# One more chunk of a sum kernel without transposes on TensorE, and two transform visits moved forward

## The chip, the cores and the metric

One core of a Trainium2 chip. The metric is the device time of one execution in microseconds; lower is better. TensorE is written PE (its weight loads PEld), VectorE DVE, ScalarE ACT, GpSimd POOL. SP only issues DMA transfers.

## The reference

Everything is float32, S = 2048 rows, D = 448 columns, F = 1792. Cut to what is computed:

```python
xn = layernorm(A_q)
# branch A: a state space layer
k_shift = sum_t k_pad[:, t:t+S] * shift_k[:, 3-t]      # 4 taps along the rows
kv = k_shift * v
y = irfft(rfft(kv, 2S) * rfft(ssm_k, 2S))[:S] + kv * ssm_D   # long convolution
a = xn * y
# branch B: an MLP
b = mish(xn @ w1 + b1) @ w2
out = A_q + a + b
```

## The kernel before

**The MLP.** The rows are cut into 8 chunks of 256, the 1792 features into 7 pairs of 128. One step of the MLP is a chunk and a pair: the first product g1_mm (22 matmuls, line 545) gives h transposed in PSUM, ACT makes Mish of it (L553), ACT and DVE split it into a rounded part and a residue (`ach`, L90; `acl`, L91), and two steps later the second product g2_mm (12 matmuls, L577 to L579) adds it to the chunk's two sums in PSUM. Each float32 product is made of three products of rounded parts, hence the many "hi" and "lo" tiles: `w1h`, `w1l`, `w2h`, `w2l`, `XH`, `XL`. When a chunk is done, DVE takes its sums out of PSUM (L584); the pool of these sums has two buffers, so the next chunk's second product waits for that.

**Half steps.** The program is written out in half steps s = 0, 1, 2, ... An even half step s holds the first product of step s/2, an odd one its Mish and the second product of the step two before. Chunk c takes half steps 14c to 14c + 13. All other work is hung into this row by tables: `at(s, ...)` puts it ahead of half step s, `after(s, ...)` behind it. The order within each engine is this written order, and each engine works its list off one after the other.

**Visits.** The long convolution is a two-stage transform. Its first stage, f1_mm (16 small matmuls, L155), takes one group of 128 x 2 rows at a time: 8 groups of the kernel ssm_k ("h", half steps in `H_AT`) and 8 groups of kv (half steps in `KV_AT`). Each such visit writes the same two PSUM pairs, `pq` and `pr`. Then f1_fold has ACT copy `pr` to SBUF (L161) and DVE form the sum and the difference with `pq` (L165, twice), and f1_out stores the result in scratch memory. A kv group is made ahead of its visit by four taps (L198 whole taps, L201 and L203 half taps, L208 the sums, L211 the product with v); the tap u = 2 can be made by POOL instead (L191, behind a one-element memset, L190). The whole taps, sums and folds have 128x896 elements.

**How a chunk enters.** For the chunks below `NT` (0, 1 and 2) DVE makes the statistics (L431, L434, L437), DVE or POOL normalizes (L444), PE transposes (ln_T, L497: eight transposes a chunk, four per half), and ACT and DVE split the transposed tile from PSUM into XH and XL (L509, L507). For the chunks from `NT` on the columns come already on partitions from a transposed copy of q in memory (xT_load, L459). Their statistics are made on ACT (nt_stats, L467 to L469) and finished on POOL, which stores them to memory (L475); SP loads them back, spread over all partitions, as a row of means and scales (nt_row, L478), once for each half of the chunk into one buffer; DVE normalizes with it (nt_norm, L484, twice a half), and ACT and DVE split from SBUF (nt_split, L491, L492). `NT_HOW` and `NT_STATS` say at which half steps this happens; with c the chunk they count from 14(c - 1), plus 1 for c below 5.

Of the kernel before, what the change touches and what calls it, by code (L numbers as in the profile page):

```python
# [23 lines left out]
G2_LAG = 2  # L24
H_HEAD = 1
H_AT = {2: 6, 3: 9, 0: 12, 4: 16, 5: 20, 6: 26, 7: 32}
KV_AT = (24, 29, 34, 39, 44, 50, 55, 59)
POOL_H = {20: (0, 2)}
OCT_AT = (66, 3)
I2_AT = {100: ((6, 7, 0, 1), 92, (95, 97, 98, 99), (0, 2, 0, 1)),  # L30
         108: ((2, 3, 4, 5), 101, (104, 105, 106, 107), (0, 1, 0, 1))}
LATE = 2
NT = 3
NT_AT = {"q": -5, "x": -1, "stats": -2, "flush": 0, "row": (4, 8), "norm": (7, 10), "split": (8, 11)}
NT_SOON = dict(NT_AT, row=(4, 5), norm=(4, 7), split=(6, 8))
NT_HOW = {c: dict(NT_SOON) for c in (4, 7)}
NT_HOW[6] = dict(NT_AT, row=(4, 10), norm=(8, 11), split=(9, 13))
NT_HOW[7]["x"] = 0
NT_HOW[3] = dict(NT_SOON, q=-9, stats=-3, flush=-2)
NT_HOW[5] = dict(NT_AT, q=-8, stats=-4, flush=-2)  # L40
NT_STATS = {3: 27, 4: 41, 5: 53, 6: 70, 7: 82}
EVAC_SOON = 2,
END = 288
WARM_N = (448, 448, 448)
# [4 lines left out]
def tile_kernel(ctx: ExitStack, tc, q, qT, k, v, sk, hT, sD, w10, w1, w2, c_fib, c_g, c_gi, c_i2, out):  # L49
# [20 lines left out]
    E = dp.tile([NJ * 4, 64, D], F32, name="E")  # L70
    MR = {c: dp.tile([2, CH], F32, name="MR") for c in range(NT, NCHUNK)}

# [8 lines left out]
    def rs(c):  # L81
        return rstd[:, 2 * c:2 * c + 2] if c < NT else mv[:, 2 * c:2 * c + 2, 1]

# [37 lines left out]
    def at(slot, fn, *args):  # L121
        plan.setdefault(int(slot), []).append((fn, args))

    def after(slot, fn, *args):
        plan2.setdefault(int(slot), []).append((fn, args))
# [294 lines left out]
    def xn_tile():  # L420
        return mp.tile([128, 4, CH], F32, name="xn", bufs=1)

    def ln_parts(c):
        st = mp.tile([128, 2, 6], F32, name="bst", bufs=2)
        ve = mp.tile([128, 2], F32, name="ve", bufs=2)
        if c < NT:
            XN[c] = xn = xn_tile().rearrange("p a b -> p (a b)").rearrange("p (j d) -> p j d", j=2)
# [83 lines left out]
    def ln_T(c, jj):  # L511
        if jj == 0:
            dv(len(drip))
            x_tiles(c)
        p = pg()
        transposes(c, jj, p)
        for lo in range(2):
            x_split(c, jj, p, lo)
# [87 lines left out]
    def mlp_slot(s):  # L606
# [3 lines left out]
        if half == 0:  # L610
            if i < n:
                c, p = pairs[i]
                if c + 1 < NT:
                    if p == 0:
# [8 lines left out]
        else:  # L623
            if i < n:
                c, p = pairs[i]
                if p == NP - 2 and c + 1 < NT:
                    ln_T(c + 1, 0)
# [25 lines left out]
    for g in range(-2, 0):  # L653
        at(12, k_load, g)
    for g, t in enumerate(KV_AT):
        d = t - (KV_AT[g - 1] if g else t - 6)
        at(t - d - (3 if g > 1 else 2), k_load, g)
# [51 lines left out]

    for c in range(NT, NCHUNK):  # L710
        at_ = NT_HOW.get(c, NT_AT)
        b = 2 * NP * (c - 1) + (1 if c < 5 else 0)
        at(b + at_["q"], ln_load, c)
        at(b + at_["x"], xT_load, c)
        after(NT_STATS[c], nt_stats, c)
        for jj in range(2):
# [152 lines left out]
```

## Time and profile before

| | |
|---|---|
| median of 3 runs | 357.95 us (357.68 to 358.1) |
| profiled execution | 357.3 us |
| span of its profile, first to last instruction | 355.5 us |
| granted clock of PE | 1.000 |
| busy: PE / DVE / ACT / POOL | 351.0 / 282.7 / 160.1 / 72.9 us |

In the rows of the timeline the first number is the start in us from the span's start, the second the duration; then engine, line, operation, output <- inputs, and in brackets the idle time of the engine ahead of it and what ended it. "x2" is two instructions merged into one row. SPq and ACTq are the engines' issues of DMA transfers. "DMA to landing" is the time from issue until the data is there.

### The profile page before, as it was taken

The page shows a single profiled execution, that of the slowest core. Times are in us where ns is not written, and L with a number is a line of the kernel's source. Part 1 is how long each engine was busy: PE and PEld are TensorE (multiplying, and loading weights), DVE is VectorE, ACT ScalarE, POOL GpSimd, SP SyncE. Part 2 cuts the span into 40 slices and gives each one's busy share as a digit, 9 for nine tenths or more (in the row PEclk, how much of TensorE's full clock was granted, in tenths as well). Part 3 has the DMA queues.
Part 4 walks back from the last instruction along what each step waited for, and adds up shares of the span by engine and source line. Part 5 has one row for each costly group of instructions (what it writes and reads, how often), then busy time and mean ns, then how long its engine had stood idle before and what let it go on. Part 6 is the DMA issues. An engine that isn't in the chain of part 4 may idle for free.

```text
span 355.5 us, 7510 instructions
## 1 busy us (share of the span) xinstructions
PE 351.0 (99%) x3098; PEld 289.9 (82%) x3098; DVE 282.7 (80%) x376; ACT 160.1 (45%) x308; POOL 72.9 (21%) x83
## 2 busy tenths in 40 slices
PE   8999999999999999999999999999999999999996
PEld 2988888888888989888987568658757699979795
DVE  5989748998999998997539868868985963788943
ACT  4966552347343643373232732333634333354480
POOL 2037002822210250222000120110310116040030
PEclk9999999999999999999999999999999999999999
DMA  7999976949769446664969389779756466999076
GB/s 255 337 387 296 406 301 168 350 116 249 211 178 314 126 151 176 217 162 83 270 211 353 109 310 288 248 233 381 247 176 225 105 170 235 407 350 282 26 115 145
DMA packets 30835, 83.27 MB, mean 234 GB/s; under 512 B 3153, under 2 KB 15954, under 8 KB 30802
## 3 DMA queue, kind: packets, MB, share of 16 engines
q1 hardware_dynamic: 21842, 47.67, 39.8%
q0 software_dynamic: 4928, 22.95, 20.2%
q10 hardware_dynamic: 4032, 12.18, 12.9%
q8 instruction: 24, 0.39, 0.4%
q14 instruction: 9, 0.07, 0.1%
HBM read 54.34 MB, written 28.45 MB: 233 GB/s over the span
## 4 chain that ended last, share of the span: by engine, by line
PE 99%; DVE 0%; issue 0%
PE pg L545 24%; PE pg L577 13%; PE pg L579 13%; PE pg L578 12%; PE pa L545 6%; PE pq L545 5%; PE pq L155 4%; PE pa L299 3%; PE pr L545 3%; PE pq L244 3%; PE pr L244 3%; PE pp L545 2%; PE pa L244 1%; PE pg L733 1%; PE pg L497 1%; PE pp L353 1%
## 5 line engine op out<-in xcount | busy, mean ns | idle before, releaser
L577 PE MATMUL pg<-w2h,ach 128*128 128x448 f32 x222 | 81.5, 367 | 0.0
L579 PE MATMUL pg<-w2h,acl 128*128 128x448 f32 x222 | 80.6, 363 | 0.0
L578 PE MATMUL pg<-w2l,ach 128*128 128x448 f32 x222 | 80.4, 362 | 0.0
L91 DVE TENSOR_TENSOR acl<-a,ach 128x512 fp32r<-128x512 f32 x56 | 38.9, 694 | 33.9 <-ACT ach L90 33.8
L545 PE MATMUL pg<-XH,w1h 128*128 128x256 f32 x264 | 52.6, 283 | 0.0
L553 ACT ACTIVATE a<-pg,b1t 128x256 f32<-128x256 f32 x66 | 27.8, 471 | 54.4 <-PE pg L545 43.5
L577 PEld LDWEIGHTS pg<-w2h,ach 128*128 128x128 f32 x222 | 41.6, 187 | 9.4 <-issue 5.0
L545 PEld LDWEIGHTS pg<-XH,w1h 128*128 128x128 f32 x264 | 41.4, 188 | 6.9 <-issue 5.6
L579 PEld LDWEIGHTS pg<-w2h,acl 128*128 128x128 f32 x222 | 41.7, 188 | 2.5
L578 PEld LDWEIGHTS pg<-w2l,ach 128*128 128x128 f32 x222 | 41.7, 188 | 2.3
L545 PE MATMUL pg<-XL,w1h 128*128 128x256 f32 x264 | 42.9, 277 | 0.0
L165 DVE TENSOR_TENSOR st<-pq,st 128x896 f32<-128x896 f32 x32 | 34.8, 1089 | 4.9 <-ACT st L161 4.1
L545 PEld LDWEIGHTS pg<-XL,w1h 128*128 128x128 f32 x264 | 35.9, 188 | 0.0
L90 ACT CAST ach<-a 128x512 fp32r<-128x512 f32 x56 | 34.8, 621 | 1.7
L545 PE MATMUL pg<-XH,w1l 128*128 128x256 f32 x198 | 33.7, 278 | 0.0
L191 POOL TENSOR_TENSOR x<-kr,skb 128x896 f32<-128x896 f32 x8 | 17.0, 2129 | 70.2 <-PE pr L155 26.1
L310 POOL DMA_DIRECT2D E<-qe x14 | 8.8, 631 | 94.4 <-ACT qe L253 94.4
L208 DVE TENSOR_TENSOR x<-x 128x896 f32<-128x896 f32 x24 | 26.2, 1091 | 2.0 <-POOL x L191 1.4
L545 PEld LDWEIGHTS pg<-XH,w1l 128*128 128x128 f32 x198 | 27.6, 188 | 0.2 <-DVE w1l L395 0.2
L161 ACT COPY st<-pr 128x896 f32<-128x896 f32 x16 | 14.5, 908 | 13.7 <-PE pr L155 11.5
L553 ACT ACTIVATE a<-pa,b1t 128x256 f32<-128x256 f32 x16 | 6.7, 471 | 30.4 <-PE pa L545 30.4
L155 PE MATMUL pq<-x,con 32*64 32x448 f32 x128 | 15.9, 560 | 0.0
(186 smaller groups left out, 646.8 us busy)
## 6 DMA issues: line engine op xcount, KB each, us to landing
Dkv<-st ACTq DMA_DIRECT2D x16, 448.0 KB, 5.0
ah<-Dh SPq DMA_DIRECT2D x8, 896.0 KB, 6.9
av<-Dkv SPq DMA_DIRECT2D x8, 896.0 KB, 9.4
e<-E POOLq DMA_DIRECT2D x8, 896.0 KB, 7.4
E<-qe POOLq DMA_DIRECT2D x14, 448.0 KB, 7.0
kr<-in_k_dram SPq DMA_DIRECT2D x10, 448.0 KB, 6.2
Dh<-st ACTq DMA_DIRECT2D x10, 448.0 KB, 6.8
x<-in_hT_dram SPq DMA_DIRECT2D x8, 448.0 KB, 6.4
```

The source lines that it names most:

```text
L90: nc.scalar.copy(h, raw)
L91: V.tensor_sub(l, raw, h)
L155: nc.tensor.matmul(ps[h][64 * jj:64 * jj + 64, b, :D], f1[rg:rg + 32], x[rg:rg + 32, jj], start=True, stop=True, tile_position=(rg, 64 * jj))
L165: f(st[:, n], e, st[:, 1])
L191: nc.gpsimd.tensor_mul(o, KR[g - u // 2], skb[:, u:u + 1].to_broadcast([128, 2, D]))
L208: V.tensor_add(KV[g], KV[g], o)
L244: nc.tensor.matmul(bk(p, r)[32 * t:32 * t + 32, :D], g[rs, t, c], a[rs, t], start=True, stop=True, tile_position=(64 * r, 32 * t))
L545: nc.tensor.matmul(ps[n], l, r, start=all(m[0] != n for m in seq[:n_]), stop=all(m[0] != n for m in seq[n_ + 1:]))
L553: nc.scalar.activation(a[:, n], ps[n], AF.Mish, bias=b1t[:, 2 * p + n:2 * p + n + 1])
L577: nc.tensor.matmul(ps, ah[:, n, cs], w2h[:, f], start=f == 0, stop=False)
L578: nc.tensor.matmul(ps, ah[:, n, cs], w2l[:, f], start=False, stop=False)
L579: nc.tensor.matmul(ps, al[:, n, cs], w2h[:, f], start=False, stop=f == NF - 1 or (f == NF - 3 and jj == 1 and c == NCHUNK - 1))
```

## The change

Chunk 2 joins the chunks without transposes (`NT = 2`), with half steps of its own: q loaded ahead of 10, statistics behind 13, columns loaded ahead of 16, the two rows ahead of 16 and 20, normalized behind 18 and 21, split behind 19 and 23. The first kv visit goes from half step 24 to 22, the second from 29 to 28, and their loads, taps, folds and stores go with them.

```diff
-KV_AT = (24, 29, 34, 39, 44, 50, 55, 59)
+KV_AT = (22, 28, 34, 39, 44, 50, 55, 59)
 POOL_H = {20: (0, 2)}
...
-NT = 3
+NT = 2
...
+NT_HOW[2] = dict(NT_AT, q=-5, x=1, row=(1, 5), norm=(3, 6), split=(4, 8))
 NT_HOW[6] = dict(NT_AT, row=(4, 10), norm=(8, 11), split=(9, 13))
...
-NT_STATS = {3: 27, 4: 41, 5: 53, 6: 70, 7: 82}
+NT_STATS = {2: 13, 3: 27, 4: 41, 5: 53, 6: 70, 7: 82}
```

The added line makes all line numbers behind it one higher in the changed kernel (L155 becomes L156).

On ACT, behind the Mish of step 6 (half step 13), before (`pg` is a first product's PSUM tile, `Dh` the scratch memory of the kernel groups):

```order
L553 ACTIVATE a<-pg_549,b1t 128x256 x2
L90 CAST ach<-a 128x512
L176 DMA Dh<-st 64x2x896 x2
L553 ACTIVATE a<-pg_597,b1t 128x256 x2
L90 CAST ach<-a 128x512
L90 CAST w2h<-x 128x896
L161 COPY st<-pr 128x896
```

and now:

```order
L554 ACTIVATE a<-pg_552,b1t 128x256 x2
L91 CAST ach<-a 128x512
L468 ACTIVATE a,bst<-qt 128x448
L469 ACTIVATE mv<-bst 128x1
L470 ACTIVATE a,bst<-qt,mv 128x448
L468 ACTIVATE a,bst<-qt 128x448
L469 ACTIVATE mv<-bst 128x1
L470 ACTIVATE a,bst<-qt,mv 128x448
L177 DMA Dh<-st 64x2x896 x2
L554 ACTIVATE a<-pg_612,b1t 128x256 x2
L91 CAST ach<-a 128x512
L91 CAST w2h<-x 128x896
```

Chunk 2's statistics came in ahead of a store and the Mish of step 7.

On DVE, from the evacuation of chunk 0's second sum (half step 18) to the fold of kernel group 5 (`st<-pq`, half step 20), before:

```order
L584 TENSOR_TENSOR qt<-pg_307,qt 128x448
L201 TENSOR_TENSOR x<-kr,skb 128x448
L431 BN_STATS bst<-qt 128x6
L203 TENSOR_TENSOR x<-kr,skb 128x448
L431 BN_STATS bst<-qt 128x6
L208 TENSOR_TENSOR x<-x 128x896
L434 BN_AGGR mv<-bst 128x2
L91 TENSOR_TENSOR acl<-a,ach 128x512
L434 BN_AGGR mv<-bst 128x2
L190 MEMSET x 1x1
L165 TENSOR_TENSOR st<-pq,st 128x896
```

and now:

```order
L585 TENSOR_TENSOR qt<-pg_308,qt 128x448
L199 TENSOR_TENSOR x<-kr,skb 128x896
L209 TENSOR_TENSOR x<-x 128x896
L485 TENSOR_TENSOR xn<-xn,con 128x4x128 x2
L92 TENSOR_TENSOR acl<-a,ach 128x512
L202 TENSOR_TENSOR x<-kr,skb 128x448
L204 TENSOR_TENSOR x<-kr,skb 128x448
L209 TENSOR_TENSOR x<-x 128x896
L212 TENSOR_TENSOR x<-x 128x896
L493 TENSOR_TENSOR XL<-xn,XH 128x4x128
L191 MEMSET x 1x1
L166 TENSOR_TENSOR st<-pq,st 128x896 x2
```

The rest of the first kv group (its tap u = 2 now on DVE) and the first half of chunk 2 stand ahead of the fold. Ahead of the evacuation the tap u = 1 of that group (L202, L204, L209) has come in as well, behind the fold of kernel group 4.

On PE, at the end of half step 21 and the beginning of 22, before:

```order
L579 MATMUL pg_754<-w2h,acl 128x448
L545 MATMUL pg_840<-XH,w1h 128x256 x3
L545 MATMUL pg_840<-XH,w1l 128x256 x3
L545 MATMUL pg_840<-XH,w1h 128x256
L545 MATMUL pg_840<-XL,w1h 128x256 x4
```

and now:

```order
L580 MATMUL pg_768<-w2h,acl 128x448
L156 MATMUL pq<-x,con 64x448 x2
L156 MATMUL pr<-x,con 64x448 x2
L156 MATMUL pq<-x,con 64x448 x2
L156 MATMUL pr<-x,con 64x448 x2
L546 MATMUL pg_870<-XH,w1h 128x256 x3
```

The first kv visit stands ahead of the first product of step 11, one pair behind the visit of kernel group 5.

## The prediction

> **What bounds the kernel now.** I read the engines' busy line and the chain on the page first, then what TensorE (PE) waited for.
>
> ```profile
> PE 351.0 (99%) x3098; PEld 289.9 (82%) x3098; DVE 282.7 (80%) x376; ACT 160.1 (45%) x308; POOL 72.9 (21%) x83
> PE 99%; DVE 0%; issue 0%
> PE pg L733 <- DVE wz L729: 1.0, 1, 1.0
> ```
>
> The whole chain is PE, and PE waits once, for 1.0 us at the start. So the time is the length of PE's own list: whatever leaves it is gained in full, and a wait put into it is lost in full. The list can be timed in the chain in order of time (start, duration, pieces of one line merged):
>
> ```profile
> 54.13 2.51 PE pg L545 x22
> 59.04 0.52 PE pq L155 x2
> 65.10 2.51 PE pg L545 x22
> 70.01 0.52 PE pq L155 x2
> 70.95 2.72 PE pg L545 x22
> 73.67 0.44 PE pg L497 x4
> 77.46 0.59 PE pg L497 x4
> 78.05 2.60 PE pg L545 x22
> 83.05 2.52 PE pg L545 x22
> 94.12 0.52 PE pq L155 x2
> ```
>
> Read with the half steps: 54.13 is the first product of half step 18, 59.04 the visit of kernel group 5 in 20, 65.10 half step 22, 70.01 the first kv visit in 24, and 73.67 and 77.46 the transposes of chunk 2. A pair without extras takes 59.04 - 54.13 = 4.91 us.
>
> **What leaves PE's list.** The first four transposes are 0.44. The second four come right behind a visit: 0.59 + 2.60 against the plain 2.72 at 70.95 makes 0.47. Sum -0.91. The second kv visit stood in an odd half step (29); 83.05 to 94.12 is 11.07, less two pairs (9.82) 1.25. In an even one a visit costs 65.10 - 59.04 - 4.91 = 1.15. It goes from 29 to 28, so -0.10; the first goes from 24 to 22, even to even, 0. In all -1.01 us, provided that PE never waits.
>
> **What the change puts before PE.** The two PSUM pairs pq and pr serve every visit, and a visit can start only when ACT has copied pr and DVE has read pq twice (L165). Kernel group 5 fills them at 59.04 in half step 20. Today DVE empties them next, and the kv visit comes two pairs later:
>
> ```profile
> 42.00 2.21 DVE L165 TENSOR_TENSOR st<-pq,st 128x896 f32<-128x896 f32 x2 [2.11 <-ACT st L161]
> 44.13 0.68 DVE L91 TENSOR_TENSOR acl<-a,ach 128x512 fp32r<-128x512 f32 x1
> 47.23 0.69 DVE L91 TENSOR_TENSOR acl<-a,ach 128x512 fp32r<-128x512 f32 x1 [2.42 <-ACT ach L90]
> 54.91 1.15 DVE L584 TENSOR_TENSOR qt<-pg,qt 128x448 f32<-128x448 f32 x2
> 55.97 0.61 DVE L201 TENSOR_TENSOR x<-kr,skb 128x448 f32<-128x448 f32 x1
> 61.03 1.09 DVE L165 TENSOR_TENSOR st<-pq,st 128x896 f32<-128x896 f32 x1 [1.10 <-ACT st L161]
> 62.16 1.09 DVE L165 TENSOR_TENSOR st<-pq,st 128x896 f32<-128x896 f32 x1
> ```
>
> The banks are free at 63.25 and wanted at 70.01: 6.8 us of room. After the change they are wanted at 65.10, and DVE reaches that fold only behind the rest of the kv taps, chunk 2's first normalization and its split. So I add up DVE's list from the first instruction that the change delays. The steps from start to start come from a stretch where DVE runs without gaps:
>
> ```profile
> 107.13 1.09 DVE L208 TENSOR_TENSOR x<-x 128x896 f32<-128x896 f32 x1
> 108.14 0.68 DVE L91 TENSOR_TENSOR acl<-a,ach 128x512 fp32r<-128x512 f32 x1
> 108.74 0.62 DVE L201 TENSOR_TENSOR x<-kr,skb 128x448 f32<-128x448 f32 x1
> 109.28 0.62 DVE L203 TENSOR_TENSOR x<-kr,skb 128x448 f32<-128x448 f32 x1
> 109.93 1.09 DVE L208 TENSOR_TENSOR x<-x 128x896 f32<-128x896 f32 x1
> 111.06 1.09 DVE L211 TENSOR_TENSOR x<-x 128x896 f32<-128x896 f32 x1
> 112.06 0.68 DVE L492 TENSOR_TENSOR XL<-xn,XH 128x512 fp32r<-128x512 f32 x1
> 112.67 1.41 DVE L484 TENSOR_TENSOR xn<-xn,con 128x512 f32<-128x512 f32 x2
> 113.99 0.69 DVE L91 TENSOR_TENSOR acl<-a,ach 128x512 fp32r<-128x512 f32 x1
> ```
>
> That is 1.01 for a whole tap or a sum, 0.60 for a residue (acl), 0.54 and 0.65 for the two half taps, 1.13 for a sum that the next one waits for, 1.00 for the product with v, 0.61 for a split, 1.32 for a normalization.
>
> The delay begins on ACT. Chunk 2's statistics now stand on it between the Mish of pair 6 and the stores and Mish of pair 7. Their price is chunk 3's, the same rows in the same place:
>
> ```profile
> 42.74 0.62 ACT L90 CAST ach<-a 128x512 fp32r<-128x512 f32 x1
> 45.71 0.84 ACT L553 ACTIVATE a<-pg,b1t 128x256 f32<-128x256 f32 x2 [2.35 <-PE pg L545]
> 82.90 0.58 ACT L467 ACTIVATE a<-qt 128x448 f32<-128x448 f32 x1 [0.73 <-DVE st L165]
> 86.15 0.19 ACT L469 ACTIVATION_READ_ACCUMULATOR a<-qt,mv 128x1 f32 x1
> 86.26 0.63 ACTq L176 DMA_DIRECT2D Dh<-st  x1
> 86.99 0.84 ACT L553 ACTIVATE a<-pg,b1t 128x256 f32<-128x256 f32 x2 [0.65 <-PE pr L155]
> ```
>
> From 82.90 to 86.99 statistics, two stores and the way to the next Mish take 4.09 (the 0.65 ahead of the last row is put down to PE, but the issue of the second store fills it to 86.89). From 43.3 (the end of 42.74 + 0.62) that gives Mish 7 at 47.4 instead of 45.7. The residue follows a Mish by 47.23 - 45.71 = 1.52, so DVE takes it up at 48.9. Its idle time before 47.23 hides nothing, because every later instruction stands behind this one. Then:
> - residue 0.60, tap 1.01, w2 residue 1.01 (same shape), fold of group 4 2.13 (42.00 to 44.13), half taps and sum 2.20, residue 0.60: 56.45. Here chunk 0's sums are taken out of PSUM (L584), 1.5 us later than today's 54.91; the first is done at 57.1, and pair 7's second product wants its bank at 54.13 + 2.51 = 56.64. PE waits some 0.5 us here, and the bigger wait below swallows it.
> - the two sums 1.06 (54.91 to 55.97), the whole tap again 1.1 (DVE now reaches it before POOL's copy in half step 20, which is still made and used by nobody), sum 1.01: 59.6.
> - normalization 1.32, residue 0.60, half taps 1.19, sum 1.13, product with v 1.00, split 0.61, memset 0.15: 65.6.
> - fold of group 5, 2.21: 67.8.
>
> With 0.1 for the release the first kv visit starts at 67.9 instead of 65.10: +2.8 us. The normalization must also find its row of means in SBUF:
>
> ```profile
> 94.14 0.33 SPq L478 DMA_DIRECT2D con<-MR  x1
> DMA to landing us min/median/max: 5.8/5.8/5.8
> DMA to landing us min/median/max: 3.2/4.8/10.6
> ```
>
> Chunk 3's row was issued 94.14 - 86.34 = 7.8 us after its statistics (two POOL instructions, the store, its landing) and landed after 5.8; all ten took 3.2 to 10.6. For chunk 2 that is statistics to 46.75, issue at 54.55, landing at 57.8 to 65.1, wanted at 59.6: a wait of 0 to 5.5. By the median 4.8 it is 0, by the nearest row, which also runs beside a store, 0.75; I take 0.4.
>
> Sum: -1.01 + 2.8 + 0.4 = +2.2 us. The bounds: if the statistics held nobody up, 1.7 less (+0.1 without the row); if the row takes longest, up to 5.1 more.
>
> What I cost at nothing: POOL loses chunk 2's normalization, off the path. The later folds: the next visit is half step 26, 11 us on, when DVE has 7 us of work for that bank. SP holds kernel group 6 and v 1 behind the second row, for which it must wait until about 61 (norm 0); they are wanted in 26 and 28, more than 15 us later. XH and XL of chunk 2 are done near 77, wanted in half step 28 near 86. The closest cover is the load of k 0:
>
> ```profile
> 35.76 0.46 SPq L181 DMA_DIRECT2D kr<-in_k_dram  x1
> DMA to landing us min/median/max: 13.0/13.0/13.0
> ```
>
> It landed at 48.8 in a crowded stretch, and the first tap now wants it at 49.5. In the queue it changes places with the load of kernel group 5, and the new 512 KB of columns stand behind it, so I leave it at nothing; what it is later than 49.5 comes on top one for one.
>
> The sum stands against the profiled execution, 357.3 us (span 355.5); the median of the runs is 357.95, so 359.5 there and 360.15 for the median.
>
> [...] In this trace the granted clock is full throughout and PE never stands longer than 1.0 us, so no row shows what a long stop costs. [...]
>
> **Rivals.**
> 1. Not slower: DVE reaches group 5's fold in time. Place: the fold before half step 22; it decides if the fold ends by 66.0, 1.8 us earlier than I add up. For it speaks that DVE idles 2.42 us before 47.23 and could hold more there; against it that this idle time waits for a Mish which moves later. If it ends by 65.0, all of -1.01 is kept: 356.9.
> 2. ACT's statistics do not hold up Mish 7 (they start earlier or cost less): +0.1, 358.1.
> 3. The row lands late, as the slowest of ten did: DVE stands for up to 5.5 us in front of the normalization, PE as long behind it. +3.5 to +7: 361.5 to 365.
> 4. The clock halves behind the stop. One pair at half speed would cost another 4.91: up to 365.
>
> **Chances.** Forecast, +1.2 to +3.5: 0.60. Rival 1: 0.11. Rival 2, between -0.2 and +1.2: 0.15. Rival 3: 0.11. Rival 4: 0.03. The range 357.8 to 361.6 leaves out most of rivals 1, 3 and 4; the forecast's own is 359.2 to 361.4. About 0.2% (0.7 us) is what a measurement can tell here. Faster takes rival 1 without its weak end: 0.09. Same takes that end and most of rival 2: 0.15. Slower: 0.76.
>
> **What would show it.** L498 (497 before) with 16 transposes instead of 24; PE waiting on L166 for 1.5 to 3 us near 66 to 68, and on L585 near 57; DVE busy without a gap from 49 to 68; ACT's Mish 7 near 47.4. I am wrong if PE starts the first kv visit near 65 (then the time falls by about 1 us), if DVE stands in front of L485 for microseconds (row), or if another wait shows behind half step 28.

## The result and the profile after

| | before | after |
|---|---|---|
| median of 5 runs, same chip | 357.68 us (357.15 to 358.1) | 363.73 us (362.40 to 364.27) |
| profiled execution, its span | 357.3, 355.5 us | 364.18, 362.4 us |
| granted clock of PE, mean | 1.000 | 0.990 |

The ratio is 1.0164 [1.0148, 1.0181]: slower by 6 us, where 2.2 had been forecast, and outside the range.

First what PE waited for (in all, times, longest), then the page's busy line and its chain:

```profile
PE pq L156 <- DVE st L166: 4.4, 1, 4.4
PE pg L734 <- DVE wz L730: 1.0, 1, 1.0
PE pg L761 <- DVE ve L438: 0.4, 1, 0.4
PE 352.3 (97%) x3090; PEld 290.5 (80%) x3090; DVE 285.7 (79%) x376; ACT 163.4 (45%) x318; POOL 66.2 (18%) x81
PE 84%; DMA 8%; DVE 2%; POOL 2%; ACT 1%; issue 1%; SPq 0%; ACTq 0%; DVEq 0%; POOLq 0%
```

One wait is new and large, at the place that the prediction named (the other two lie in the first 6 us), and DMA stands in a chain that was all PE. The busy time of PE rose by 1.3 us (351.0 before), though it does 8 matmuls fewer: some of them ran slower. The chain in order of time shows both:

```profile
46.56 0.73 POOL mv L472
47.59 8.41 DMA MR<-mv
56.02 5.54 DMA con<-MR
61.68 0.70 DVE xn L485
...
67.63 1.02 DVE st L166
68.67 1.10 DVE st L166
69.82 1.01 PE pq L156 x2
71.62 4.54 PE pg L546 x22
```

It runs through chunk 2's row: the means are stored at 47.59 and land 8.41 later, the row is loaded at 56.02 and lands after 5.54, then DVE normalizes, makes the taps, folds kernel group 5 (L166), and only then comes the first kv visit (69.82). Its first matmuls took 1.01 where they took 0.52 before, and the 22 of the first product behind it 4.54 instead of 2.72. The clock column of four stretches shows why (columns: us, then busy us of PE, its weight loads, DVE, ACT and POOL, granted clock, DMA share, GB/s):

```profile
62.00:65.40 3.40, 3.40 (x21) 2.89 (x19) 3.33 (x6) 2.24 (x5) 0.00 (x0) 1.00 0.41 117
65.40:68.65 3.25, 0.00 (x0) 0.00 (x0) 3.20 (x5) 0.55 (x1) 0.78 (x1) 1.00 0.93 283
68.65:75.50 6.85, 5.68 (x34) 4.29 (x35) 6.76 (x10) 0.91 (x1) 1.61 (x2) 0.50 0.72 202
75.50:78.00 2.50, 2.50 (x16) 2.38 (x15) 1.89 (x3) 1.77 (x4) 1.79 (x1) 1.00 0.92 340
```

PE stands from 65.40 to 69.82. From 68.65 its clock is granted at half, and stays there for 6.85 us, 5.68 of which have PE at work.

And DVE's list, in which the fold stands:

```profile
55.98 1.15 DVE L585 TENSOR_TENSOR qt<-pg,qt 128x448 f32<-128x448 f32 x2
57.05 1.08 DVE L199 TENSOR_TENSOR x<-kr,skb 128x896 f32<-128x896 f32 x1
58.17 1.09 DVE L209 TENSOR_TENSOR x<-x 128x896 f32<-128x896 f32 x1
61.68 1.42 DVE L485 TENSOR_TENSOR xn<-xn,con 128x512 f32<-128x512 f32 x2 [2.42 <-DMA con<-MR]
...
68.67 1.09 DVE L166 TENSOR_TENSOR st<-pq,st 128x896 f32<-128x896 f32 x1
```

DVE stands for 2.42 us ahead of the normalization, waiting for the row. Without that the fold would have ended at 69.76 - 2.42 = 67.34, and PE would have stood from 65.40 to about 67.4: 2.0 us.

**The account.** In the trace of before the visit of half step 34 starts at 100.18, after at 106.56: 6.38 later. 0.30 of it is there already at the visit of half step 20 (59.27 against 58.97). PE's stop from 65.40 to 69.82 adds 4.42. The visit and the product behind it take 69.82 to 76.16 = 6.34, while the same two take 65.25 to 68.90 = 3.65 at full clock (run 9 below): 2.69 for the clock. Less 1.01 for the work that left PE, as it was forecast: 0.30 + 4.42 + 2.69 - 1.01 = 6.40. From there on nothing is added: DVE's last instruction starts 6.31 later than before (358.53 against 352.22). The rest of the 6.9 us between the two profiled spans lies behind it, in the last stores.

### The profile page after: what moved, and what is told of

It is laid out like the page before. It is cut to its first block, busy times and chain, and to the rows that moved or that the text cites. A ratio compares the mean times of both kernels' runs of the same rounds, so it can differ in the third digit from the quotient of the medians.

```text
span 362.4 us, 7512 instructions
## 1 busy us (share of the span) xinstructions
PE 352.3 (97%) x3090; PEld 290.5 (80%) x3090; DVE 285.7 (79%) x376; ACT 163.4 (45%) x318; POOL 66.2 (18%) x81
## 4 chain that ended last, share of the span: by engine, by line
PE 84%; DMA 8%; DVE 2%; POOL 2%; ACT 1%; issue 1%; SPq 0%; ACTq 0%; DVEq 0%; POOLq 0%
PE pg L546 19%; PE pg L578 11%; PE pg L580 11%; PE pg L579 10%; PE pa L546 6%; PE pq L546 5%; PE pq L156 3%; PE pa L300 3%; PE pr L546 3%; PE pr L245 3%; PE pq L245 3%; DMA Dh<-st 3%; DMA MR<-mv 2%; PE pp L546 2%; DMA x<-in_hT_dram 2%; DMA con<-MR 2%
## 5 line engine op out<-in xcount | busy, mean ns | idle before, releaser
L92 DVE TENSOR_TENSOR acl<-a,ach 128x512 fp32r<-128x512 f32 x56 | 39.8, 710 | 35.1 <-ACT ach L91 35.1
L546 PE MATMUL pg<-XH,w1h 128*128 128x256 f32 x264 | 53.7, 287 | 0.0
L546 PEld LDWEIGHTS pg<-XH,w1h 128*128 128x128 f32 x264 | 42.3, 192 | 9.0 <-issue 7.7
L166 DVE TENSOR_TENSOR st<-pq,st 128x896 f32<-128x896 f32 x32 | 34.9, 1090 | 5.0 <-ACT st L162 4.1
L209 DVE TENSOR_TENSOR x<-x 128x896 f32<-128x896 f32 x24 | 26.2, 1091 | 1.9 <-POOL x L192 1.2
L156 PE MATMUL pq<-x,con 32*64 32x448 f32 x128 | 16.7, 586 | 4.6 <-DVE st L166 4.4
```

Of the source, the lines that this page charges most:

```text
L92: V.tensor_sub(l, raw, h)
L156: nc.tensor.matmul(ps[h][64 * jj:64 * jj + 64, b, :D], f1[rg:rg + 32], x[rg:rg + 32, jj], start=True, stop=True, tile_position=(rg, 64 * jj))
L166: f(st[:, n], e, st[:, 1])
L209: V.tensor_add(KV[g], KV[g], o)
L546: nc.tensor.matmul(ps[n], l, r, start=all(m[0] != n for m in seq[:n_]), stop=all(m[0] != n for m in seq[n_ + 1:]))
```

## The experiments

In the expectations theory A is the one of the prediction, widened by what the profile after showed: DVE reaches the fold of kernel group 5 too late, for chunk 2's row and normalization stand ahead of it, and the clock falls behind the stop. Theory B differs from run to run; in the first three it puts the cost into the visits that were moved. Each ratio is to the kernel before on the same chip. The runs stand on several chips, on which the kernel before takes 357.4 to 357.7 us, so gains against the changed kernel are taken from each one's distance to the kernel before.

**1. The visits back, chunk 2 as changed**

```diff
-KV_AT = (22, 28, 34, 39, 44, 50, 55, 59)
+KV_AT = (24, 29, 34, 39, 44, 50, 55, 59)
```

> The change with both kv visits back at half steps 24 and 29; chunk 2 still enters without transposes. Theory A (PE waits for DVE's list, and that list is held up by the late row of means): undoing the visits does not bring the gain back. DVE reaches the normalization near 58.5, waits until the row lands near 61.6, and everything behind it is late: the kv product is done near 71.4 while PE wants it at 70.0 (wait about 1.5 us), and the fold of kv 0 near 79.5 while PE wants its banks at 77.5 (wait about 2 us). Both waits are shorter than the one after the change, so no drop of the clock. Sum -0.9 + 3.5 = +2.6 us, about 360.3. Theory B (the early visit alone makes the wait): no wait is left, -0.9 us, about 356.8.

Measured: 360.88 us (359.45 to 362.25), ratio 1.0109 [1.0073, 1.0144]: near A's 360.3, far from B's 356.8. PE waits at the two places that A named, 0.9 us at the first kv visit for its product with v (L212) and 1.7 at the next visit for the fold of kv 0. The visit comes two half steps later, but the taps were moved with it, and DVE still stands for the row:

```profile
PE pq L156 <- DVE st L166: 1.7, 1, 1.7
PE pq L156 <- DVE x L212: 0.9, 1, 0.9
DVE xn L485 <- DMA con<-MR: 2.4, 1, 2.4
```

The four executions fall into two groups: 359.45 and 359.81 at a mean clock of 1.0 and 0.998, 361.95 and 362.25 at 0.995. A had ruled out a drop of the clock, and that part failed in two of four.

**2. The visits moved, chunk 2 as before**

```diff
-NT = 2
+NT = 3
```

> Only the visits are moved (22 and 28); chunk 2 is transposed as before. Theory A: without row, statistics on ACT, normalization and split ahead of it the fold of kernel group 5 ends near 66.4 on DVE, where PE wants the banks at 65.0: a wait of about 1.4 us, clock full; less 0.1 for the even half step, +1.3 us, about 359.0. Theory B (the early visit alone): the wait stays near 4.4 us and the clock drops behind it: +6 us, about 363.7.

Measured: 359.12 us (358.81 to 359.24), ratio 1.0046 [1.0031, 1.0061]: the time that A gave, but by a place of which only a part had been expected. PE waits 0.3 us for the fold and 0.9 us for chunk 2's split (L508), which now comes late behind the taps. So the earlier visits cost 1.7 us by themselves, through DVE's order, and the larger part of the 6 us needs chunk 2.

**3. Chunk 2's row, normalization and split behind the fold**

```diff
-row=(1, 5), norm=(3, 6), split=(4, 8)
+row=(1, 7), norm=(5, 8), split=(6, 9)
```

> The change with chunk 2's normalization behind half steps 20 and 23 and its split behind 21 and 24, so that the fold of kernel group 5 stands ahead of them on DVE. Theory A: the fold ends near 65.4, PE wants it at 65.3, wait 0.1 to 0.2 us; what was pushed back makes the fold of kernel group 6 end near 83.1, wanted near 82.4, wait up to 0.8; clock full. Sum -1.0 + 0.2 + 0.0 to 0.8: -0.8 to 0 us, 356.9 to 357.7. Theory B (the visit is too early whatever stands ahead of the fold): still over 2 us of wait, 359 or more.

Measured: 358.13 us (356.78 to 359.78, 10 runs), ratio 1.0018 [1.0003, 1.0033]. Three entries of a table bring the changed kernel from 6.05 us above the kernel before to 0.73: 5.3 of the 6 us. PE's waits in the profile:

```profile
PE pg L579 <- DVE w2l L92: 1.0, 1, 1.0
PE pq L156 <- DVE st L166: 0.6, 1, 0.6
PE pg L578 <- DVE qt L585: 0.4, 1, 0.4
```

At the first kv visit nothing is left of the 4.4 us. The 0.6 stands at the second one (85.40), which waits for the fold of kernel group 6, as expected. The other two waits come earlier, at 53.52 and 58.98; the profiled execution is the slowest of the ten. The time is 0.4 to 1.2 above what was expected: the forecast gain of 1 us does not appear. Where it went is taken up in runs 7 to 9.

**4. PE kept at work during the stop**

Five matmuls in float32 (ten in the profile) into a bank that nobody reads, ahead of half step 22; DVE's list is as it was.

```diff
+HOLD = 5
...
+    def hold_array():
+        p = pg()
+        for _ in range(HOLD):
+            nc.tensor.matmul(p[0:64, 0:448], f1, skb[:, 0], start=True, stop=True)
...
+    plan.setdefault(22, []).insert(0, (hold_array, ()))
```

> The change with five float32 matmuls of 448 columns, whose result nobody reads, on PE ahead of the first kv visit, where it stands still for 4.4 us. Theory A with the clock: they fill some 4 us of the wait, the release comes when it came (near 69.7), the granted clock stays at 1.00, and the visit and first product behind it take 3.7 us instead of 6.2: about 2.5 us less than the change, 361.2. Theory C (they are slow because transfers and POOL work beside them, not for the clock): they stay slow, the time stays at 363.7.

Measured: 361.05 us (360.58 to 362.24), ratio 1.0106 [1.0085, 1.0127], with the clock near 1.0 (0.998 to 1.0) in all four. The chain, the end of the fold on DVE and two stretches of this kernel:

```profile
66.47 3.90 PE pg L643 x10
70.38 0.52 PE pq L157 x2
71.31 2.71 PE pg L547 x22
68.57 1.09 DVE L167 TENSOR_TENSOR st<-pq,st 128x896 f32<-128x896 f32 x1
66.40:70.30 3.90, 3.90 (x11) 1.29 (x10) 3.87 (x6) 0.00 (x0) 2.08 (x1) 1.00 1.00 384
70.30:74.00 3.70, 3.70 (x40) 2.99 (x40) 3.67 (x6) 0.91 (x1) 0.00 (x0) 1.00 0.49 128
```

The visit starts even later than in the changed kernel (70.38 against 69.82), but takes 0.52 instead of 1.01, and the product behind it 2.71 instead of 4.54. Visit and product together take 74.02 - 70.38 = 3.64 us, 2.70 less than the 6.34 of the changed kernel, which is the 2.69 of the account. The matmuls that nobody needs last 0.7 us longer than the wait would have, since the fold ends at 69.66; that is lost again. Against the kernel before the time is 3.65 us more, where the change was 6.05: a gain of 2.4. So the 2.7 us are the clock's, and the clock falls because PE stands: with PE at work and the visit no earlier, it stays.

**5. The row without its round trip**

Chunk 2's two rows are read from a fixed place of the input at once, so chunk 2's normalized values mean nothing here; the instructions, their sizes and their queue are the same.

```diff
-nc.sync.dma_start(idr, MR[c][jj].partition_broadcast(128))
+nc.sync.dma_start(idr, (q[0, jj, :CH] if c == 2 else MR[c][jj]).partition_broadcast(128))
```

> The change, but chunk 2's two rows are read from fixed inputs instead of from the stored statistics, so the first row is in SBUF long before DVE comes to it; the result of chunk 2 is meaningless, all instructions and transfers stay. Theory A: DVE does not stop in front of the normalization, the fold of kernel group 5 ends near 67.3, PE waits about 2.0 us, too short for the clock to drop: -1.0 + 2.1 = +1.1 us, about 358.6. Theory B (the row matters little, DVE's work ahead of the fold makes the wait and the clock drops anyway): 362 or more.

Measured: 360.55 us (358.36 to 361.25, 6 runs), ratio 1.0067 [1.0042, 1.0093]. DVE no longer waits for a row, and PE stands 1.8 us, where A had expected 2.0. Two executions, 358.36 and 358.85, agree with the 358.6; the other four, 360.54 to 361.25, have a mean clock of 0.994 to 0.995, which A had ruled out. That 2.0 us are too short for the clock to drop was an estimate, and the runs did not bear it out. The profile is one of these:

```profile
PE pq L156 <- DVE st L166: 1.8, 1, 1.8
65.64:67.39 1.75, 0.00 (x0) 0.00 (x1) 1.72 (x3) 0.00 (x0) 1.75 (x1) 1.00 0.98 375
67.40:68.70 1.30, 1.30 (x19) 0.60 (x20) 1.30 (x2) 0.20 (x1) 0.10 (x1) 1.00 0.85 345
68.75:72.10 3.35, 3.35 (x18) 3.35 (x17) 3.28 (x6) 0.66 (x1) 0.00 (x0) 0.50 0.78 185
72.20:75.00 2.80, 2.80 (x18) 2.65 (x17) 2.77 (x5) 1.98 (x4) 2.13 (x1) 1.00 0.93 255
```

PE was at work again for 1.3 us when the clock fell, after a stop of only 1.75 us. Nothing on record had expected that, and it led to runs 10 to 12.

**6. The normalization behind the taps, ahead of the fold**

```diff
-row=(1, 5), norm=(3, 6), split=(4, 8)
+row=(1, 6), norm=(4, 7), split=(5, 8)
```

> The change with chunk 2's normalizations one half step later (behind 19 and 22, splits behind 20 and 23): the first now stands behind the kv product but still ahead of the fold of kernel group 5. Theory A: DVE has other work until the row lands, reaches the normalization near 63.1, fold ends near 66.8, PE waits about 1.5 us with a full clock: -1.0 + 1.5 = +0.5 us, about 358.2, and up to 0.8 more where transfers of the crowded stretch before come late. Theory B (all that counts is what stands ahead of the fold): the work is the same less a split (0.6), so the wait stays near 3.8 us and the time above 361.

Measured: 358.73 us (357.67 to 360.04, 10 runs), ratio 1.0036 [1.0021, 1.0052], within A's 358.2 to 359.0. PE stands 1.3 us for the fold, and the clock stays at 0.997 or more in all ten.

**7. and 8. POOL's tap put to use, and the columns loaded later**

Run 7 is run 3 with POOL's copy of the tap early enough to be used; run 8 is run 7 with chunk 2's 512 KB of columns four half steps later.

```diff
-POOL_H = {20: (0, 2)}
+POOL_H = {16: (0, 2)}
```

> The normalization behind the fold as in the run before, and the tap u = 2 of the first kv group on POOL behind half step 16, where it is early enough to be used, so DVE has one whole tap (1.1 us) less ahead of the fold. Theory A: the fold ends near 64.4, wanted at 65.3; the fold of kernel group 6 near 82.0, wanted near 82.3: no wait in the usual case, about -1.0 us, 356.5; up to 0.7 more where the transfers of the crowded stretch come late. Rival: POOL's tap slows DVE beside it, or something else stops PE: 357.4 or more.

> As the run with the tap on POOL, and the 512 KB of chunk 2's columns loaded ahead of half step 20 instead of 16, outside the crowded stretch of transfers (30 to 51 us). If this load makes the stores there late (on which ACT's copy, the statistics and so DVE's whole list hang), the spread over the runs shrinks and the time falls by up to 0.5 us against the run without it: 356.0 to 356.5. If not, the same time.

Measured: 357.52 us (10 runs), ratio 0.9995 [0.9984, 1.0006], and 357.65 us (10 runs), ratio 1.0001 [0.9991, 1.0011]. Run 7 misses its 356.5 by 1 us and falls to its rival, that something else stops PE. In run 8 the gain of up to 0.5 us does not come: the columns' load does not matter to the time. No wait is left at the visit, but a small one stands earlier. From run 7, DVE's row, the row of PE that waits for it, and the first product of half step 20:

```profile
56.77 1.15 DVE L585 TENSOR_TENSOR qt<-pg,qt 128x448 f32<-128x448 f32 x2
57.44 0.47 PE L578 MATMUL pg<-w2h,ach 128*128 128x448 f32 x1 [0.39 <-DVE qt L585]
61.01 0.62 PE L546 MATMUL pg<-XH,w1h 128*128 128x256 f32 x3
```

DVE takes chunk 0's sums out of PSUM at 56.77 (54.91 before), and PE's second product of pair 7 wants their bank. From the first product of half step 18 (54.39) to that of 20 it takes 61.01 - 54.39 = 6.62 us; before it was 59.91 - 53.97 = 5.94. The wait itself is 0.39 of the 0.68.

**9. A tap behind the sums**

Run 7, with the tap u = 1 of the first kv group (two half taps and their sum) behind the taking out of chunk 0's sums (L585) instead of in front of it; the length of DVE's list up to the fold is the same.

```diff
-        after(t - (2 if g else 1) - d + d * u / 4, taps, g, u)
+        after(18 if (g, u) == (0, 1) else t - (2 if g else 1) - d + d * u / 4, taps, g, u)
```

> As in the run with POOL's tap used (row, normalization and split of chunk 2 behind the fold of kernel group 5), and the second whole tap of the first kv group stands on DVE behind the taking out of chunk 0's sums (L585) instead of in front of it. Theory: of the 1.0 us expected there and not found, about 0.5 is lost at half step 19, where PE waits for L585, which the earlier taps had put from 54.91 to 56.4. With three DVE instructions (2.2 us) less in front, L585 starts before 55, PE has no wait on L585 near 57, the way from the first product of half step 18 to that of 20 is again 5.9 to 6.0 us instead of 6.4 to 6.6, and DVE's list up to the fold of kernel group 5 is as long as before, so that the first kv visit does not wait either. Time 0.5 us less than that run: ratio 0.998 to 0.9985, 356.7 to 357.0 where the kernel before takes 357.5. Rival: the loss at half step 19 comes from the statistics on ACT, which make the second Mish of pair 7 late, and not from L585; then 6.4 us stays there and the ratio is 0.9995 to 1.0005.

Measured: 356.61 us (355.87 to 357.60, 11 runs), against 357.58 before (15 runs); ratio 0.998 [0.9969, 0.9992], the ratio that was expected, and faster than both kernels, if only by 0.2%. DVE and the chain of this kernel:

```profile
54.11 1.14 DVE L585 TENSOR_TENSOR qt<-pg,qt 128x448 f32<-128x448 f32 x2
62.48 2.21 DVE L166 TENSOR_TENSOR st<-pq,st 128x896 f32<-128x896 f32 x2
54.27 2.51 PE pg L546 x22
60.12 2.72 PE pg L546 x22
65.25 0.52 PE pq L156 x2
66.18 2.72 PE pg L546 x22
```

From 54.27 to 60.12 is 5.85, as before (54.13 to 59.98 in the same view), so the loss of half step 19 was the wait for L585 and not ACT's statistics, which this run leaves in place. The first kv visit starts at 65.25, free of waits because the fold is done at 64.7. From the product of half step 20 to that of 34 it is 60.12 to 100.32 = 40.20 us, before 59.98 to 101.11 = 41.13: 0.93 of the 1.01.

**10. to 12. A stop of chosen length and nothing else**

Run 9, with the first sum of the fold of kernel group 5 made 2, 3 or 5 more times on DVE (`STALL`; `STALL_G` is 5).

```diff
+            if key == 'h' and g == STALL_G:
+                for _ in range(STALL):
+                    V.tensor_add(st[:, 0], e, st[:, 1])
```

> As in the run with the tap behind the sums (ratio 0.998), but the first sum of the fold of kernel group 5 is made three times instead of once on DVE, to the same result. Nothing else is changed, so TensorE alone stops in front of the first kv visit, by two sums less the room of 0.3 to 0.4 us: 2 x 1.06 - 0.3 = 1.8 us. Theory (a stop of under 2 us can already halve the granted clock behind it, whatever made the stop): 356.6 + 1.8, and 2.1 more in those executions in which the clock falls, 358.4 to 360.5, with the granted clock at 0.5 from about 69. [...] Rival 2 (the clock fell for another reason, the chunk's load or its stores): 358.4 and full clock here and in the two longer stops too.

> The same with four sums in place of one: a stop of 3 x 1.06 - 0.3 = 2.9 us. Theory: 356.6 + 2.9 + 2.1 to 2.5 = 361.6 to 362.0 in nearly every execution, granted clock at 0.5 for 4 to 7 us behind the stop. [...] Rival 2: 359.5, full clock.

> The same with six sums in place of one: a stop of 5 x 1.06 - 0.3 = 5.0 us, a little above the 4.4 us of the changed kernel. Theory: 356.6 + 5.0 + 2.5 = 364.1, granted clock at 0.5 for about 7 us. [...] Rival 2: 361.6, full clock.

| stop of PE in the profile | executions: us (mean clock) |
|---|---|
| 2.0 us | 359.40 (0.999); 360.34, 360.63 (0.994); 361.03 (0.995) |
| 2.8 us | 360.09 (0.999); 362.36, 362.63 (0.991); 363.55 (0.990) |
| 5.4 us | 363.93, 364.25 (0.991); 364.43 (0.989); 365.63 (0.990) |

The stop was measured in one execution of each kernel (361.03, 360.09 and 363.93). Medians 360.48, 362.50 and 364.34; ratios 1.0072 [1.0052, 1.0092], 1.0129 [1.0090, 1.0168] and 1.0196 [1.0175, 1.0218]. The theory had 358.4 to 360.5, 361.6 to 362.0 and 364.1. A stop made by DVE alone lowered the clock (to 0.50 in the profiles of 2.0 and 5.4 us), so rival 2 falls; a stop of 2.0 us did it in three of four executions (mean clock 0.994 to 0.995, against 0.997 or more in all eleven of run 9). The same kernel with 2.8 us kept its clock once and lost it three times, 2.3 to 3.5 us apart. Two rows each for 2.0 and for 5.4 us (in the stop, then the low clock with PE at work), and one behind the stop of 2.8 us that kept its clock:

```profile
65.45:67.47 2.02, 0.00 (x1) 0.00 (x1) 1.99 (x3) 0.00 (x0) 0.00 (x0) 1.00 0.91 277
69.15:72.45 3.30, 3.30 (x17) 3.30 (x17) 3.27 (x5) 1.43 (x2) 0.00 (x0) 0.50 0.32 77
65.40:68.55 3.15, 0.00 (x0) 0.00 (x0) 3.05 (x4) 0.00 (x0) 0.00 (x0) 1.00 0.70 258
70.80:75.30 4.50, 4.50 (x29) 3.10 (x30) 4.43 (x7) 1.43 (x2) 0.00 (x0) 0.50 0.15 37
68.10:70.00 1.90, 1.90 (x25) 1.20 (x26) 1.86 (x3) 0.00 (x0) 0.00 (x0) 1.00 0.02 8
```

## Why the prediction was right and wrong

**What leaves PE's list: right.** L498 has 16 transposes, and run 9, where PE waits for nothing new, gains 0.7 us by its ratio and 1.0 by its medians against the -1.01 of the sum.

**DVE's list: right in place, a little large.** Mish 7 came at 46.92 (47.4 forecast), chunk 0's sums at 55.98 (56.45), and without the row the fold would have ended at 67.34 (67.8). The visit was wanted at 65.40 and not 65.10, since the whole program stood 0.3 later. So this term was 2.0 us instead of 2.8. Run 5, which takes the row away, has this wait alone: 1.8.

**The wait on L585 near 57: not in this kernel.** The sums were taken just in time. It is there, 0.2 to 0.4 us, in the runs where DVE comes to them later, and costs 0.5 to 0.7 on the way from half step 18 to 20.

**The row: a term of the sum that was mis-sized.** It was put at 0.4 us from bounds of 0 to 5.5, and measured 2.42. That DVE would stand in front of L485 for microseconds was one of the prediction's own signs of being wrong. The landing of the row itself was forecast well (5.54 against 5.8). What was wrong is the time from the statistics to the issue of the row, 7.8 us by chunk 3: here it was 56.02 - 46.21 = 9.8, because the store of the means took 8.41 to land. What ran beside it (first chunk 3's store in the kernel before, 84 to 96 us, then chunk 2's after, 38 to 58 us, then run 8, same stretch):

```profile
DMA packets 806, 2.49 MB, mean 207 GB/s; under 512 B 113, under 2 KB 113, under 8 KB 806
MR<-mv POOLq DMA_DIRECT2D x1, 2.0 KB, 5.7
DMA packets 1821, 6.39 MB, mean 320 GB/s; under 512 B 254, under 2 KB 254, under 8 KB 1819
MR<-mv POOLq DMA_DIRECT2D x1, 2.0 KB, 8.4
DMA packets 1700, 5.75 MB, mean 287 GB/s; under 512 B 253, under 2 KB 329, under 8 KB 1698
MR<-mv POOLq DMA_DIRECT2D x1, 2.0 KB, 6.4
```

More traffic and a later landing go together, but that the one makes the other is not shown: in the changed kernel and in runs 1, 6 and 9, which load the columns in the same place, with 301 to 321 GB/s over this stretch, the store landed after 6.9 to 8.4 us, so its landing scatters by more than 1 us at much the same load. The wait for the row scatters too (2.42 in the changed kernel, 1.24 in run 4). What can be said is that a price taken from a stretch with 207 GB/s was carried into one with 320, though the prediction had called it crowded where it spoke of k 0.

**The clock: the term that was left out of the sum.** This is the largest failed step. The clock had no term in the forecast, only a rival with a chance of 0.03 and a price of up to 4.91; it fell in every run of the changed kernel (0.990 to 0.995) and cost 2.69 us in the profile. What failed is the estimate that a stop of the forecast's 2.8 us leaves the clock full; the trace of before, with no stop above 1.0 us, did not show that. Stops of 1.75 and 2.0 us, in runs 5 and 10, lowered the clock in seven of ten executions. The low stretches, read from the clock column in steps of 0.25 us, last 3.4 us behind 1.75 and 2.0 us (68.73 to 72.14 in run 5) and 6.8 with 4.4 and 5.4 us (68.66 to 75.49 in the changed kernel). The length of the stop alone does not settle it: 1.75 us was enough in four of six executions of run 5, and 2.8 us in run 11 once was not.

**Together.** The forecast's -1.01 + 2.8 + 0.4 became -1.01 + 2.0 + 2.42 + 2.69, and 0.30 that was there before. Row and clock were two rivals of the list, priced one at a time. They are one event: the late row makes the stop longer, and the longer stop brings the clock down. With the clock kept up (run 4) the median is 361.05, inside the range of 357.8 to 361.6; it is the clock that carried the time out of it. By runs 5 and 11 the forecast's own 2.0 to 2.8 us of stop would have brought it down in most executions too (run 5: 360.55 with four of six, run 11: 362.50 with three of four).

## What to carry to other kernels

Where TensorE is the bound and works without a stop, price a new wait on it by the wait plus what the clock does behind it (2.69 us in the changed kernel, 1.7 in run 5), and treat a wait of 1.75 to 2 us as able to halve the clock (runs 5 and 10). Where a wait can't be avoided, work that nobody needs can keep the clock up (run 4: 0.998 to 1.0 in all four, and 2.4 us less). When a step is moved ahead, list what stands in front of the consumer on its engine and put the instruction that waits for a transfer behind the one that the bound engine waits for: here three entries of a table were worth 5.3 us (run 3). And once the big wait is gone, look for the small ones that it covered, as run 9 did with a single tap.

## What the runs showed of the hardware

The granted clock fell to 0.50 behind stops of PE of 1.75 us (run 5) and 2.0 us (run 10), shorter than the 3.4 us for which it then stayed low. The length of a stop is known from the profiled execution of each kernel, the fall of the clock from every execution's mean: a stop of 1.3 us lowered it in none of ten executions (0.997 or more, where one low stretch makes 0.995), 1.75 to 2.0 us in seven of ten, 2.8 us in three of four, 4.4 and 5.4 us in all nine. In run 1, with stops of 0.9 and 1.7 us, it fell in two of four. In the profiles the low stretch lasted 3.4 us (runs 5 and 10) or 6.8 (the changed kernel and run 12). In runs 5 and 10 it began 1.3 and 1.6 us after PE was back at work (run 10: back at 67.47, low from 69.1); in the changed kernel and in run 12 it began 3.3 and 3.2 us into the stop. It cost 1.7 us in the profile of run 5 (visit and product 67.39 to 72.72 = 5.33 instead of 3.65). Why one execution of a kernel keeps its clock and another loses it is shown by none of the runs.
